# Writing the first stage and token block 0 out in ticks, in a one-core attention and two-MLP kernel on Trainium2

## The chip, the cores and the metric

The kernel runs on 1 core of one Trainium2 chip. The number that counts is the device time in microseconds (us) of one execution, as the median of several. The engines are TensorE (PE in the profile, with its weight loads as PEld), VectorE (DVE), ScalarE (ACT), GpSimd (POOL) and the queue engine SyncE (SP), which issues every DMA of this kernel in one row. Each engine works through its own list of instructions strictly in the order in which they stand there; engines wait for one another through semaphores.

## The reference

Three stages, one after the other, in float32 (inputs cut to what matters):

```python
# attention: q, k, v are (4 batches, 8 heads, 768 positions, 64)
k_sum = k.reshape(B, H, nb, 32, D).max(axis=3)      # 24 summary keys
v_sum = v.reshape(B, H, nb, 32, D).mean(axis=3)     # 24 summary values
scores_l = scale * q @ k^T, kept where |i - j| < 16, else -1e9
scores_s = scale * q @ k_sum^T + log(32)
a = softmax(concat[scores_l, scores_s]);  x = a @ concat[v, v_sum]
x = x.transpose(0, 2, 1, 3).reshape(3072, 512)
# first MLP: w1, w2, w3 are (512, 768), w_out is (768, 512)
x = max(max(x @ w1, x @ w2), x @ w3) @ w_out
# second MLP: w_in is (512, 2048), w_out2 is (2048, 512)
h = x @ w_in;  out = (h * tanh(softplus(h))) @ w_out2
```

The weights arrive as float64, and the kernel reads them as pairs of 32-bit words.

## The kernel before, in words

**Tokens.** The 3072 tokens are cut into 8 blocks of 384. A block is 3 attention units u (128 tokens each, two tiles of 64 queries), so block 0 is u = 0, 1, 2 and the kernel has 24 units, 6 to a batch. Block i's first MLP is 18 groups of 12 matmuls (`gemm1`: three products for each of 6 column slices f; the code calls their tiles hp, m, hh, hl) and then a part that multiplies by w_out (`gemm2`: tiles yp and y, stored to x2d).

**Precision.** Each float32 factor is split into a coarse and a fine part (xh and xl, hh and hl, two halves of each weight slot), and a product is three matmuls: coarse by coarse, coarse by fine, fine by coarse.

**Weight jobs.** The first MLP's weights are 24 pieces of 128x512 numbers. A job fetches a piece's words (`fetch`, a DMA of 512 KB into the tile words, 3 buffers), takes magnitudes on ACT (`size_of`, L177, tile wa), turns float64 words into a float32 and a rest on DVE (`narrow`, five instructions L185, L187, L190, L193, L195), rounds to the coarse part on ACT (L235), and forms the fine part. For the first 14 jobs (PEJOBS) PE adds the parts (L240 to L242, tile wp) and ACT copies the sum out (L243); for the last 10, DVE does it with two further instructions (L198 and L237). `run_job` moves the pipeline on by one: it finishes one job, fetches another, narrows a third and sizes a fourth. Jobs 1 to 18 are w1, w2, w3 by column slice; 19 to 24 are w_out.

**Attention.** A unit has five steps, made by `step(u)`: scores, row maximum and exponentials of u+1 (`s2`); a q transpose of u+2, with the preparation of keys of the next batch (`k_prep`, tiles tp, kst, ksum); first half of the transposes of u (`s3`, tiles ptp, pT) and normalisation of u+1 (`s2b`); preparation of the next batch's value means (`v_prep`, tiles vp, nat, stored to vsd) and the second half of s3; the output product of u (`s4`, tiles xp, xh, xl) and loads of keys for u+2. `KLOAD0` and `VLOAD0` say at which of batch 0's units the keys and values of batch 1 are loaded. Keys of later tiles come from a copy in DRAM, kTd, that `store_far` and `k_prep` write. The tile nat has 4 buffers, shared by q, k and v loads; y and m share one pair of buffers (tag my).

**Order.** The instructions are written in program order and a scheduler then places them on each engine by a simulated time, so two weight jobs may stand interleaved and later work may be pulled ahead. What steers it in the program is the order of the calls: the first stage runs 4 jobs among the first unit's work, and then one job after every second attention step:

```python
IB = ITEMS * BT // GT            # 15 attention steps to a block
while nstep < IB + 1:
    attend(nstep + 1)
    for _ in range(PER[nit % len(PER)]):     # PER = [1, 0]
        run_job()
    nit += 1
```

Each block's loop then takes its 22 groups one by one: in blocks 0 and 1 it calls `run_job` before each while there are jobs, then emits the group, then calls `attend(IB * (i + 1) + (IB * (n_ + 1)) // G + (AHEAD * min(n_ + 1, 8)) // 8)`, so that attention stands up to 19 steps beyond block i's own (AHEAD is 4) when the block ends.

Of the kernel before, what the change touches and what calls it, by code (L numbers as in the profile page):

```python
# [33 lines left out]
ITEMS = 5  # L34
PER = [1, 0]
AHEAD = 4
# [17 lines left out]
def tile_kernel(ctx, tc, q, k, v, w1, w2, w3, w_out, w_in2, w_out2, out):  # L54
# [88 lines left out]
    last = {"early": True}  # L143

# [53 lines left out]

    fetched, sized, narrowed = [], [], []

    def run_job(after=None):

        if narrowed:
            w, rest, done = narrowed.pop(0)
            done(w, rest)
        if jobs:
            src, done, parts = jobs.pop(0)
            fetched.append((fetch(src), done, parts))  # L210
        if sized:
            words, a, done, parts = sized.pop(0)
            narrowed.append((*narrow(words, a, parts), done))
        if fetched and (len(fetched) > 1 or not jobs):
            words, done, parts = fetched.pop(0)
            with tc.issue_after(after) if after else nullcontext():
                a = size_of(words)
            sized.append((words, a, done, parts))

    def busy():  # L220
        return bool(jobs or fetched or sized or narrowed)

# [5 lines left out]
    def into(tag, place, key):  # L228
        def done(w, rest):
            if tag not in slot_of:  # L230
                slot_of[tag] = wslot(tag)
            t = slot_of[tag]
            wa[key] = t, 2 * place
            h, l = t[:, 2 * place], t[:, 2 * place + 1]
            nc.scalar.copy(h, w)  # L235
            if rest is None:
                nc.vector.tensor_tensor(out=l, in0=w, in1=h.bitcast(F32), op=ALU.subtract)  # L237
                return
            sums = gps.tile([P, 512], F32, name="wp", tag="g")
            nc.tensor.matmul(sums, lhsT=ident, rhs=w, start=True, stop=False)  # L240
            nc.tensor.matmul(sums, lhsT=one_r, rhs=rest, start=False, stop=False)
            nc.tensor.matmul(sums, lhsT=neg_r, rhs=h, start=False, stop=True)  # L242
            nc.scalar.copy(l, sums)  # L243

        return done
# [13 lines left out]
    def keep(f, i):  # L259
        def done(w, _):  # L260
            h = stage.tile([P, 512], F32R, name="wr", tag="wr", bufs=AB)
            nc.scalar.copy(h, w)
            nc.vector.tensor_tensor(out=w, in0=w, in1=h.bitcast(F32), op=ALU.subtract)
            nc.sync.dma_start(out=w2d[f][:, 2 * i], in_=h.bitcast(F32))
            last["store"] = nc.sync.dma_start(out=w2d[f][:, 2 * i + 1], in_=w)

        return done
# [166 lines left out]

    def s2(u):

        t = u % NG
        kind = "first" if t == 0 else "last" if t == NG - 1 else "mid"
        mask = masks[kind]
        sc = [bank("sc") for r in range(2)]  # L440
# [8 lines left out]
        for p in range(NP):  # L449
            for e in reversed(range(GT)):  # L450
                for r in range(2):
                    d = slice(r * D, (r + 1) * D)
                    c = slice(e * QT, (e + 1) * QT)
                    nc.tensor.matmul(
                        sc[r][c, p, 0:KX], lhsT=qT[u % RQ][d, p, c], rhs=kT[(GT * u + e) % RK][d, p],
                        start=add, stop=add or p == NP - 1,
                    )
        s = ap2.tile([P, H, KX], F32, name="s", tag="s", bufs=SB)
        src = [x[:, :, 0:KX] for x in sc]
        if add:  # L460
# [10 lines left out]
        sm = ap2.tile([P, H], F32, name="esum", tag="esum")  # L471
        for h in range(H):
            r, p = divmod(h, NP)
            nc.scalar.activation(  # L474
                out=s[:, h], in_=src[r][:, p], func=AF.Exp, bias=nm[:, r, p : p + 1], accum_out=sm[:, h : h + 1]
            )
        rs = ap2.tile([P, H, 1], F32, name="rs", tag="rs")
        att_t[u] = (s, sm, rs)

# [44 lines left out]
    VLOAD = {0: [0], 1: [1], 2: [2], 3: [3, 4, 5], 4: [6, 7]}  # L524
    KLOAD0 = {1: [0, 1], 2: [2, 3], 3: [4, 5]}
    VLOAD0 = {1: [0], 2: [1], 3: [2], 4: [3, 4, 5]}

    def step(u):
# [5 lines left out]
        def first():  # L534
            if u == 1:
                store_far()
            for T in (GT * (u + 1), GT * (u + 1) + 1):
                if ok(u + 1):
                    load_v(T)
            if ok(u + 1):  # L540
                s2(u + 1)

        def second():
            if ok(u + 2):
                q_prep(*divmod(u + 2, NG))
            for g in more and kload.get(t - 1) or ():
                k_prep(b + 1, g)
            if ok(u + 3):
                load_nat("q", q, *divmod(u + 3, NG))
            for g in more and kload.get(t) or ():  # L550
                load_nat("k", k, b + 1, g)
# [7 lines left out]
        def fourth():  # L559
# [5 lines left out]
            for g in more and vload.get(t) or ():  # L565
                if b:
                    load_vsum(b + 1, *VP[g])
                else:
                    load_nat("v", v, 1, g)
            s3(u, 1)  # L570

        def fifth():
            s4(u)
            for T in (GT * (u + 2), GT * (u + 2) + 1):
                if ok(u + 2):
                    load_k(T)
# [47 lines left out]
    def gemm2(i, e):  # L624
# [14 lines left out]

        return [emit]  # L640


# [117 lines left out]
    vroom = [r[:, j].rearrange("p (h d) -> p h d", h=H) for r in vroom for j in range(4)]  # L760
    for g in range(NG):
        nat["k", 0, g] = t = room[g].rearrange("p (h d) -> p h d", h=H)
        nc.sync.dma_start(out=t, in_=k[0, :, g * P : (g + 1) * P, :].rearrange("h p d -> p h d"))
        if g == 2:
            load_nat("q", q, 0, 0)
    run_job()
    for g in range(NG):
        nc.sync.dma_start(out=vroom[g], in_=v[0, :, g * P : (g + 1) * P, :].rearrange("h p d -> p h d"))
        if g == 2:
            run_job()  # L770
    load_nat("q", q, 0, 1)
    for g in range(NG):
        k_prep(0, g, kst[g])
    for T in range(RK):
        load_k(T)
    q_prep(0, 0)
    run_job()
    s2(0)
    load_v(0)
    load_v(1)  # L780
    s2b(0)
    q_prep(0, 1)
    run_job()
    load_nat("q", q, 0, 2)
    vp = aps.tile([P, H, D], F32, name="vp", tag="a")
    for g in range(NG):
        mean_v(vp[0:NB].rearrange("p h d -> p (h d)"), vroom[g], g * NS, NB, g == 0, g == NG - 1)
    nc.scalar.copy(vr[0][0:NB], vp[0:NB])
    for t in vr[1:]:
        nc.gpsimd.tensor_copy(t[0:NB], vr[0][0:NB])  # L790

    steps = [it for u in range(NU) for it in step(u)]
    nstep = nit = 0

    def attend(upto):
        nonlocal nstep
        while nstep < min(upto, len(steps)):
            steps[nstep]()
            nstep += 1

    IB = ITEMS * BT // GT
    while nstep < IB + 1:
        attend(nstep + 1)
        for _ in range(PER[nit % len(PER)]):
            run_job()
        nit += 1

# [30 lines left out]
    early = 0  # L838
    for i in range(NBLK):
        groups = []  # L840
# [57 lines left out]
```

## Time and profile before

| what | value |
|---|---|
| median of 3 runs | 1119.14 us (1119.0 to 1120.24) |
| the profiled execution's own time | 1121.29 us |
| its span, first to last instruction | 1119.5 us |
| mean granted TensorE clock | 0.991 |
| PE busy | 1087.2 us, 97% of the span |
| DVE busy | 816.1 us, 73% |
| ACT busy | 548.6 us, 49% |
| DMA moved | 125.49 MB |

A timeline row reads: start in us, length in us, engine, line, operation, output<-inputs, shapes, count, and in brackets the idle time ahead of it with what ended it. A row of the table by stretches gives the busy time, with the number of instructions, of each engine. Matmul rows overlap, since matmuls are pipelined, so a matmul's price is the distance between starts. A PE that counts as busy isn't PE at its peak.

### The profile page before, as it was taken

The numbers are of one execution on the slowest core, as the hardware profiler recorded it, in microseconds if no ns is written. First come the engines' busy times: TensorE is split into PE (matmuls) and PEld (weight loads), VectorE is DVE, ScalarE is ACT, GpSimd is POOL, SyncE is SP. The second block draws the span as 40 slices with busy tenths as digits, with TensorE's granted clock in tenths as the row PEclk, the third lists the DMA queues.
The fourth block names the chain that finished last, engine by engine and source line by source line (L and its number), as shares of the span: only waits on it lengthen the run. The fifth ranks groups of instructions, "written<-read, shape, count | busy, mean of one in ns | idle before, by whom it ended". The sixth has DMA issues, their size and how long they took to land.

```text
span 1119.5 us, 18658 instructions
## 1 busy us (share of the span) xinstructions
PE 1087.2 (97%) x7004; PEld 986.9 (88%) x7004; DVE 816.1 (73%) x1623; ACT 548.6 (49%) x1336; POOL 77.4 (7%) x132
## 2 busy tenths in 40 slices
PE   6789989999999999999999999999999999999998
PEld 3468879999999899999999999989899998999987
DVE  5788953377887898942247887887878778787775
ACT  4676543345544555532135554545545454554543
POOL 3000021211114100100000000000000000000000
PEclk8989999999999999999999999999999999999999
DMA  9898772467888877412646010101001010000000
GB/s 239 199 248 230 170 193 63 136 155 197 247 224 253 200 228 190 152 37 71 233 178 248 20 37 1 57 1 29 29 1 58 1 44 14 15 29 1 29 1 29
DMA packets 179730, 125.49 MB, mean 112 GB/s; under 512 B 125048, under 2 KB 161400, under 8 KB 177592
## 3 DMA queue, kind: packets, MB, share of 16 engines
q1 hardware_dynamic: 179640, 124.30, 39.9%
q8 instruction: 55, 0.90, 0.3%
q14 instruction: 35, 0.29, 0.1%
HBM read 88.05 MB, written 35.05 MB: 110 GB/s over the span
## 4 chain that ended last, share of the span: by engine, by line
PE 75%; DVE 11%; ACT 6%; DMA 4%; issue 2%; SPq 1%; POOL 1%; ACTq 0%; POOLq 0%; DVEq 0%
PE up L692 8%; PE up L690 8%; PE acc L745 8%; PE up L691 8%; PE acc L746 8%; PE acc L747 8%; PE hp L599 5%; PE hp L600 5%; PE hp L601 5%; ACT s L474 3%; PE yp L633 2%; PE yp L634 2%; PE yp L635 2%; DMA kT<-kTd 1%; DVE words L190 1%
## 5 line engine op out<-in xcount | busy, mean ns | idle before, releaser
L708 ACT ACTIVATE r<-n,two 128x384 f32<-128x384 f32 x128 | 78.9, 616 | 155.3 <-DVE n L705 155.3
L599 PE MATMUL hp<-xh,a 128*128 128x384 f32 x384 | 133.6, 348 | 2.0 <-ACT y L637 2.0
L600 PE MATMUL hp<-xl,a 128*128 128x384 f32 x384 | 129.5, 337 | 0.0
L601 PE MATMUL hp<-xh,a 128*128 128x384 f32 x384 | 129.3, 337 | 0.0
L731 DVE TENSOR_TENSOR gl<-g,gh 128x384 fp32r<-128x384 f32 x128 | 71.4, 557 | 64.7 <-ACT gh L730 64.1
L701 ACT ACTIVATE e<-up 128x384 f32<-128x384 f32 x128 | 62.9, 492 | 97.3 <-PE up L692 96.6
L474 ACT ACTIVATE s<-s,nm 128x120 f32<-128x120 f32 x168 | 64.0, 383 | 45.1 <-DVE nm L467 45.1
L599 PEld LDWEIGHTS hp<-xh,a 128*128 128x128 f32 x384 | 72.7, 189 | 4.7 <-ACT y L637 2.4
L718 DVE TENSOR_TENSOR p<-up,r 128x384 f32<-128x384 f32 x128 | 70.5, 551 | 6.2 <-ACT r L709 6.2
L600 PEld LDWEIGHTS hp<-xl,a 128*128 128x128 f32 x384 | 72.7, 189 | 0.8 <-issue 0.5
L601 PEld LDWEIGHTS hp<-xh,a 128*128 128x128 f32 x384 | 72.7, 189 | 0.0
L723 DVE SCALAR_TENSOR_TENSOR g<-u,n 128x384 f32<-128x384 f32 x128 | 70.8, 553 | 0.9
L703 DVE TENSOR_SCALAR ep<-e 128x384 f32<-128x384 f32 x128 | 45.9, 358 | 34.8 <-ACT e L701 34.3
L721 DVE SCALAR_TENSOR_TENSOR u<-u,p 128x384 f32<-128x384 f32 x128 | 70.6, 552 | 0.4
L705 DVE SCALAR_TENSOR_TENSOR n<-e,ep 128x384 f32<-128x384 f32 x128 | 70.7, 552 | 0.3
L720 DVE SCALAR_TENSOR_TENSOR u<-n,r 128x384 f32<-128x384 f32 x128 | 70.2, 548 | 0.0
L730 ACT CAST gh<-g 128x384 fp32r<-128x384 f32 x128 | 64.2, 502 | 9.7 <-DVE g L723 9.7
L633 PE MATMUL yp<-hh,c 128*128 128x384 f32 x192 | 65.4, 346 | 3.5 <-ACT hh L618 1.9
L709 ACT ACTIVATE r<-r 128x384 f32<-128x384 f32 x128 | 67.1, 524 | 0.9
L599 PE MATMUL hp<-xh,b 128*128 128x384 f32 x192 | 67.4, 351 | 0.0
L611 DVE TENSOR_TENSOR m<-hp,m 128x384 f32<-128x384 f32 x48 | 26.5, 553 | 53.4 <-PE hp L601 48.7
L692 PE MATMUL up<-x2h,a 128*128 128x384 f32 x192 | 64.6, 337 | 0.0
(171 smaller groups left out, 2920.3 us busy)
## 6 DMA issues: line engine op xcount, KB each, us to landing
words<-in_moe_w_out SPq DMA_DIRECT2D x22, 512.0 KB, 4.5
words<-in_moe_w SPq DMA_DIRECT2D x18, 512.0 KB, 5.2
words<-in_moe_w_in SPq DMA_DIRECT2D x16, 512.0 KB
w2d<-wr SPq DMA_DIRECT2D x32, 256.0 KB, 2.7
w2d<-wa SPq DMA_DIRECT2D x32, 256.0 KB, 4.1
kT<-kTd SPq DMA_DIRECT2D x35, 192.0 KB, 5.1
vr<-in_v SPq DMA_DIRECT2D x35, 192.0 KB, 5.2
nat<-in_q SPq DMA_DIRECT2D x24, 256.0 KB, 4.5
```

The lines of the kernel that those rows point to most:

```text
L474: nc.scalar.activation(out=s[:, h], in_=src[r][:, p], func=AF.Exp, bias=nm[:, r, p : p + 1], accum_out=sm[:, h : h + 1])
L599: nc.tensor.matmul(pt[:, :n], lhsT=wh, rhs=xh[:, c, :n], start=(c == 0), stop=False)
L600: nc.tensor.matmul(pt[:, :n], lhsT=wh, rhs=xl[:, c, :n], start=False, stop=False)
L601: nc.tensor.matmul(pt[:, :n], lhsT=wl, rhs=xh[:, c, :n], start=False, stop=(c == KC - 1))
L633: nc.tensor.matmul(pt[:, :n], lhsT=wh, rhs=hh[:, :n], start=(f == 0), stop=False)
L690: nc.tensor.matmul(pt[:, :N2], lhsT=wh, rhs=xh[:, c], start=(c == 0), stop=False)
L691: nc.tensor.matmul(pt[:, :N2], lhsT=wh, rhs=xl[:, c], start=False, stop=False)
L692: nc.tensor.matmul(pt[:, :N2], lhsT=wl, rhs=xh[:, c], start=False, stop=(c == KC - 1))
L708: nc.scalar.activation(out=r, in_=d["n"], func=AF.Ln, bias=two[:, 0:1])
L745: nc.tensor.matmul(o, lhsT=gh[:, c], rhs=w[:, 2], start=(f == 0), stop=False)
L746: nc.tensor.matmul(o, lhsT=gh[:, c], rhs=w[:, 3], start=False, stop=False)
L747: nc.tensor.matmul(o, lhsT=gl[:, c], rhs=w[:, 2], start=False, stop=(f == NF2 - 1))
```

## The change

The first stage and block 0 are written out by hand. A new context, `in_order`, links every instruction on an engine to the one traced before it on that engine, so inside it the scheduler may not reorder; it holds from the first load up to the end of block 0 (SP's DMAs included). A weight job is split into five calls: `fetch_next`, `size_next`, `narrow_next`, `round_next` (coarse part, and PE's sum where there is one) and `close_next` (fine part), and `s2` into `scores`, `largest` and `exps`. In the first stage these stand between single attention steps: 5 jobs are narrowed before the tick loop, in which block 0's remaining 21 pieces of work (three groups of gemm1 stand ahead of the loop) are taken one to a tick, with one `run_job` and some attention steps before each. Block 0's second product is cut by f, not by output slice (`gemm2_slices`), so that each slice needs one w_out job. `attend` ends block 0 at step 30. Loads of batch 1's keys and values start one unit later, and `in_order` ends before block 1, whose loop is as it was.

```diff
+    @contextmanager
+    def in_order():
+        traced = nc.cur_bb.bb.instructions
+        n = len(traced)
+        yield
+        latest = {}
+        for i in traced[n:]:
+            if i.engine in latest:
+                tc.add_manual_dep(
+                    i, latest[i.engine].name,
+                    mybir.DependencyInfo(mybir.DependencyClass.NoSync, mybir.DependencyReason.DATA),
+                    reason="in_order",
+                )
+            latest[i.engine] = i
...
     def run_job(after=None):
+        old = bool(narrowed)
+        if old:
+            round_next()
+        fresh = bool(fetched)
+        fetch_next()
         if sized:
+            narrow_next()
+        late = old and rounded[0][1]
+        if old and not late:
+            close_next()
+        if fresh:
             with tc.issue_after(after) if after else nullcontext():
+                size_next()
+        if late:
+            close_next()
...
-    VLOAD0 = {1: [0], 2: [1], 3: [2], 4: [3, 4, 5]}
+    KLOAD0 = {2: [0, 1], 3: [2, 3], 4: [4, 5]}
+    VLOAD0 = {2: [0], 3: [1], 4: [2], 5: [3, 4, 5]}
...
                     load_nat("v", v, 1, g)
+            if u == NG - 1:
+                for g in VLOAD0[t]:
+                    v_prep(1, g)
             s3(u, 1)
...
+    def gemm2_slices(i):
+        def part(f):
+            if f == 0:
+                pts.extend(gps.tile([P, 512], F32, name="yp", tag="g") for e in range(KC))
+            w, at = wa[4, f]
+            hh, hl = hhl[i, f]
+            for e, pt in enumerate(pts):
+                wh, wl = w[:, at, e * P : (e + 1) * P], w[:, at + 1, e * P : (e + 1) * P]
+                nc.tensor.matmul(pt[:, :n], lhsT=wh, rhs=hh[:, :n], start=(f == 0), stop=False)
+                nc.tensor.matmul(pt[:, :n], lhsT=wh, rhs=hl[:, :n], start=False, stop=False)
+                nc.tensor.matmul(pt[:, :n], lhsT=wl, rhs=hh[:, :n], start=False, stop=(f == NF1 - 1))
+                if f == NF1 - 1:
+                    y = g2.tile([P, MAXT * QT], F32, name="y", tag="my", bufs=2)
+                    nc.scalar.copy(y[:, :n], pt[:, :n])
+                    nc.sync.dma_start(out=x2d[i][:, e, :], in_=y[:, :n])
...
+    with in_order():
...
+        round_next()
+        s4(2)
+        scores(3)
+        first_groups = [g for f in range(NF1) for g in gemm1(0, f)] + gemm2_slices(0)
+        first_groups.pop(0)()
+        narrow_next()
+        largest(3)
+        close_next()
+        exps(3, 0)
+        exps(3, 1)
+        first_groups.pop(0)()
...
+        s2b(3)
+        first_groups.pop(0)()
+        nstep = IB
+        tick = 0
+        while first_groups:
+            if busy():
+                run_job()
+            attend(IB + (tick * IB) // 22)
+            first_groups.pop(0)()
+            tick += 1
+        attend(2 * IB)
...
-    for i in range(NBLK):
+    for i in range(1, NBLK):
```

Three places show how instructions moved. The first is DVE in the middle of block 0, in the weight jobs (wa, words and wr are a job's tiles, m and hl the MLP's). Before:

```order
L185 TENSOR_SCALAR wa<-wa 128x512
L187 TENSOR_SCALAR wa<-wa 128x512
L611 TENSOR_TENSOR m<-hp,m 128x384
L366 TENSOR_REDUCE ksum<-tp 128x4x4
L190 SCALAR_TENSOR_TENSOR words<-words,wa 128x512
L185 TENSOR_SCALAR wa<-wa 128x512
L193 TENSOR_SCALAR wa<-words 128x512
L187 TENSOR_SCALAR wa<-wa 128x512
L195 SCALAR_TENSOR_TENSOR wa<-words,wa 128x512
```

and in the change, from the loop's first ticks:

```order
L674 TENSOR_TENSOR m<-hp,m 128x384
L678 TENSOR_TENSOR hl_746<-m,hh_745 128x384
L200 TENSOR_SCALAR wa<-wa 128x512
L202 TENSOR_SCALAR wa<-wa 128x512
L205 SCALAR_TENSOR_TENSOR words<-words,wa 128x512
L208 TENSOR_SCALAR wa<-words 128x512
L210 SCALAR_TENSOR_TENSOR wr<-words,wa 128x512
L200 TENSOR_SCALAR wa<-wa 128x512
```

The five instructions of one job, which had another job's or other work between them, now stand in a row, and hl stands right behind the m that it is made from. The second place is the DMA queue. Before, in the middle of block 0, the last loads of batch 1's values stood among the weight fetches:

```order
L303 DMA nat<-in_v 128x8x64
L368 DMA kTd_175<-kst 512x1x128
L303 DMA nat<-in_v 128x8x64
L167 DMA words<-in_moe_w_out 128x1024
L318 DMA vsd_179<-nat 4x8x64
L368 DMA kTd_175<-kst 512x1x128
L303 DMA nat<-in_v 128x8x64
```

and in the change, at the end of block 0 (x2d takes block 0's result y):

```order
L182 DMA words<-in_moe_w_out 128x1024
L182 DMA words<-in_moe_w_in 128x4x256
L719 DMA x2d_182<-y 128x384 x4
L358 DMA vsd_179<-nat 4x8x64
L343 DMA nat<-in_v 128x8x64 x3
L358 DMA vsd_179<-nat 4x8x64
```

The three loads moved behind block 0's four stores. The third place is ACT where block 0 ends and block 1 begins. Before:

```order
L474 ACTIVATE s,esum<-s,nm 128x120 x8
L637 COPY y<-yp 128x384 x2
L496 COPY pT<-ptp 120x512 x2
L363 COPY kst<-tp 128x512
L637 COPY y<-yp 128x384 x2
L607 COPY m<-hp 128x384
```

and in the change:

```order
L272 CAST c_1558<-wa 128x512
L549 COPY pT<-ptp 120x512
L718 COPY y<-yp 128x384 x4
L357 COPY nat<-vp 4x512 x4
L549 COPY pT<-ptp 120x512
L570 CAST xh<-xp 128x4x128
L666 COPY m<-hp 128x384
```

Between y and the first m of block 1 there now stand four value means, a transpose copy and the last xh of block 1's input. PE has the same row there: the last slice's yp matmuls, then vp x4, ptp, xp, and then hp, block 1's first product.

More of the change, by code (lines that the diff above doesn't have):

```diff
@@ L2 @@
 import struct
[L3 removed]
+from contextlib import ExitStack, contextmanager, nullcontext
 import concourse.bass as bass
@@ L199, in narrow, with fetch_next @@
         return a, None
[L201 to L207, printed above, removed]
+    fetched, sized, narrowed, rounded = [], [], [], []
+    def fetch_next():
         if jobs:
@@ L210, in run_job, with size_next, narrow_next, round_next @@
             fetched.append((fetch(src), done, parts))
-        if sized:
[L212 to L215, printed above, removed]
+    def size_next():
+        words, done, parts = fetched.pop(0)
+        sized.append((words, size_of(words), done, parts))
+    def narrow_next():
+        words, a, done, parts = sized.pop(0)
+        narrowed.append((*narrow(words, a, parts), done))
+    def round_next():
+        w, rest, done = narrowed.pop(0)
+        rounded.append((done(w, rest), rest is not None))
+    def close_next():
+        rounded.pop(0)[0]()
+    def run_job(after=None):
+        old = bool(narrowed)
[3 more added lines that the diff above has]
+        fetch_next()
+        if sized:
+            narrow_next()
[3 more added lines that the diff above has]
+        if fresh:
             with tc.issue_after(after) if after else nullcontext():
-                a = size_of(words)
-            sized.append((words, a, done, parts))
+                size_next()
+        if late:
+            close_next()
     def busy():
-        return bool(jobs or fetched or sized or narrowed)
+        return bool(jobs or fetched or sized or narrowed or rounded)
     jobs = []
@@ L242, in done @@
             nc.tensor.matmul(sums, lhsT=neg_r, rhs=h, start=False, stop=True)
-            nc.scalar.copy(l, sums)
+            return lambda: nc.scalar.copy(l, sums)
         return done
@@ L545, in second @@
                 q_prep(*divmod(u + 2, NG))
-            for g in more and kload.get(t - 1) or ():
+            for g in more and not (b == 0 and t == NG - 1) and kload.get(t - 1) or ():
                 k_prep(b + 1, g)
@@ L573, in fifth @@
             s4(u)
+            if b == 0 and t == NG - 2:
+                for g in KLOAD0[t]:
+                    k_prep(1, g)
             for T in (GT * (u + 2), GT * (u + 2) + 1):
@@ L640, in gemm2 @@
         return [emit]
+    def gemm2_slices(i):
+        n = sizes[i] * QT
+        pts = []
+        def part(f):
[12 more added lines that the diff above has]
+                    nc.sync.dma_start(out=x2d[i][:, e, :], in_=y[:, :n])
+        return [lambda f=f: part(f) for f in range(NF1)]
     N2 = 384
@@ L760, in tile_kernel @@
     vroom = [r[:, j].rearrange("p (h d) -> p h d", h=H) for r in vroom for j in range(4)]
[L761 to L790, printed above, removed]
     steps = [it for u in range(NU) for it in step(u)]
-    nstep = nit = 0
+    nstep = 0
     def attend(upto):
```

145 lines of the change are left out of this document (123 added, 22 removed).

## The prediction

> **What bounds the kernel now.** I read the slices of the span first: they show where PE isn't full.
>
> ```profile
> PE   6789989999999999999999999999999999999998
> ```
>
> A slice is 28 us, so the time that a new order can win back lies in the first six slices; after them PE is busy and sets the pace. Next, three PE rows: block 0's first product, the last matmuls of its second product, and block 1's first product.
>
> ```profile
> 71.74 0.34 PE L599 MATMUL hp<-xh,a 128*128 128x384 f32 x1
> ...
> 154.27 0.96 PE L635 MATMUL yp<-hh,c 128*128 128x384 f32 x4
> 157.25 0.44 PE L599 MATMUL hp<-xh,a 128*128 128x384 f32 x1 [2.02 <-ACT y L637]
> ```
>
> Block 0 ends on PE at 155.2 and block 1 starts 2.0 later, at 157.25. From there on everything is PE's work, so the change is worth what it does to two numbers: when block 1 starts, and how much PE work is done by then. What holds block 0 back is DVE, which the stretches from 0 to 58 and from 58 to 152.6 show, first DVE alone, then the L190 step, of which each weight job has one:
>
> ```profile
> 58.00:152.60 94.60, 85.19 (x158) 0.96 0.90 209
> ...
> 0.00:58.00 58.00, 5.53 (x8) 0.94 0.89 221
> 58.00:152.60 94.60, 11.00 (x16) 0.96 0.90 209
> ```
>
> By 58 us 8 jobs are narrowed; the other 16 keep DVE at 85.2 of 94.6 us.
>
> **Part 1: when the tick loop starts.** The change has 5 jobs narrowed before its loop, and attention goes first. But PE's order has the scores of unit 3 ahead of block 0's first product, and these need keys that go out to DRAM and back. Before:
>
> ```profile
> 38.52 3.71 SPq L376 DMA_DIRECT2D kTd<-room  x4
> ...
> 54.68 1.05 PE L454 MATMUL sc<-kT,qT 64*64 64x120 f32 x32 [0.19 <-DMA kT<-kTd]
> ```
>
> The way from the first store to the scores took 16.2 us. In the change the stores stand behind the sixth fetch, which waits for job 3 to be rounded; I put them at 38 again, and the way at 12.5: between stores and key loads SP has one q load now, where two k loads and a weight fetch stood as well, some 4 us of issuing in all. Scores of unit 3: 50.5. From there one chain: the matmuls 1.05, the row maximum on DVE, eight exponentials on ACT, the normalisation, and f = 0's m and hl, with these prices:
>
> ```profile
> L467 DVE TENSOR_REDUCE nm<-s 128x8 f32<-128x960 f32 x6 | 6.9, 1144 | 0.0
> L366 DVE TENSOR_REDUCE ksum<-tp 128x16 f32<-128x512 f32 x7 | 4.8, 682 | 0.1
> L463 DVE TENSOR_TENSOR s<-sc,mask_mid 128x480 f32<-128x480 f32 x6 | 3.7, 648 | 0.0
> L485 DVE TENSOR_TENSOR s<-s,rs 128x960 f32<-128x960 f32 x3 | 3.5, 1157 | 0.1
> L518 DVE TENSOR_TENSOR xl<-xp,xh 128x512 fp32r<-128x512 f32 x5 | 3.4, 685 | 0.5 <-ACT xh L517 0.5
> ...
> L474 ACT ACTIVATE s<-s,nm 128x120 f32<-128x120 f32 x168 | 64.0, 383 | 45.1 <-DVE nm L467 45.1
> ```
>
> A score unit on DVE is 2 x 0.65 + 1.14 = 2.4, eight exponentials 3.1, the normalisation 1.5 with its two small helpers, m and hl 1.6: the loop's first job starts on DVE at 50.5 + 1.05 + 2.4 + 3.1 + 1.5 + 1.6 = 60. The ends I keep: 52 (stores at 34, landings quick) and 66 (the old 16.2, and PE at a lower clock).
>
> **Part 2: DVE in the loop.** 19 jobs are left, 9 whose parts PE adds (five DVE steps) and 10 that DVE finishes (seven). In the new order a job's steps follow one another and each needs the one before it. The trace has both kinds:
>
> ```profile
> 53.28 0.42 DVE L185 TENSOR_SCALAR wa<-wa 128x512 f32<-128x512 f32 x1
> 53.74 0.43 DVE L187 TENSOR_SCALAR wa<-wa 128x512 uint32<-128x512 uint32 x1
> 54.20 0.69 DVE L190 SCALAR_TENSOR_TENSOR words<-words,wa 128x512 uint32<-128x512 uint32 x1
> 54.92 0.43 DVE L193 TENSOR_SCALAR wa<-words 128x512 uint32<-128x512 uint32 x1
> ...
> 125.76 0.42 DVE L185 TENSOR_SCALAR wa<-wa 128x512 f32<-128x512 f32 x1
> 126.10 0.42 DVE L193 TENSOR_SCALAR wa<-words 128x512 uint32<-128x512 uint32 x1
> 126.43 0.42 DVE L187 TENSOR_SCALAR wa<-wa 128x512 uint32<-128x512 uint32 x1
> 126.77 0.68 DVE L195 SCALAR_TENSOR_TENSOR wa<-words,wa 128x512 f32<-128x512 uint32 x1
> 127.37 0.68 DVE L190 SCALAR_TENSOR_TENSOR words<-words,wa 128x512 uint32<-128x512 uint32 x1
> ```
>
> Start to start, a step that feeds the next takes 0.46 (53.28 to 53.74) or 0.72 (54.20 to 54.92); one that stands ahead of another job's step takes 0.34 (125.76 to 126.10) or 0.60 (126.77 to 127.37). So a five-step job is 0.46 + 0.46 + 0.72 + 0.46 + 0.60 = 2.7, a seven-step one 3 x 0.46 + 2 x 0.72 + 2 x 0.60 = 4.0, and the 19 are 9 x 2.7 + 10 x 4.0 = 64. Beside them stand 3 score units (7.3), 2 normalisations (3), 6 ksum (4.1), 2 xl (1.4) and the m, m, hl of 5 slices (15 x 0.55 = 8.3): 24, less a tenth for starts that overlap, 22. Together 86.
>
> The Trainium skill, in VectorE: DVE Perf Modes, "The DRAIN you can't avoid", says that a chain with a semaphore after each step takes exactly as long as one without. By that rule the new row of steps costs nothing; the rows above disagree by 0.12 a step, and the measurement decides. With the rule the sum would be 10 us lower (9 x 4 + 10 x 5 = 86 links).
>
> Three stalls come on top. The rows are a wait of hl for ACT's hh, where hl stands right behind m as it now always does, and on PE two sums of a job and two steps of a product:
>
> ```profile
> 167.44 0.56 DVE L619 TENSOR_TENSOR hl<-m,hh 128x384 fp32r<-128x384 f32 x1 [0.58 <-ACT hh L618]
> ...
> 35.62 1.07 PE L240 MATMUL wp<-words,ident 128*128 128x512 f32 x2
> ...
> 36.98 1.06 PE L240 MATMUL wp<-words,ident 128*128 128x512 f32 x2
> ...
> 98.50 0.33 PE L601 MATMUL hp<-xh,a 128*128 128x384 f32 x1
> 98.67 0.33 PE L599 MATMUL hp<-xh,a 128*128 128x384 f32 x1
> ```
>
> Five times 0.58 is 2.9. Once hh stands on ACT behind unit 4's eight exponentials, which take 3.1 and start as m does: 2.9 more. And in the first nine ticks PE is the longer one: 12 matmuls at 0.17 make 2.1, a job's sum takes 1.4 (35.62 to 36.98), and attention in those ticks, by the prices of Part 4, is near 0.8 a tick: 4.3, against 2.7 + 0.55 + 0.75 = 4.0 on DVE: 9 x 0.3 = 2.7. I take 8.5 for the three (ends 0 and 14). The last fine part waits for its rounding (0.7), and the last slice is 12 matmuls (2.1). End of block 0 on PE: 60 + 86 + 8.5 + 0.7 + 2.1 = 157.3, against 155.2: **+2.1**. The early start buys nothing because DVE has three more jobs ahead of it and dearer ones.
>
> **Part 3: from block 0's end to block 1's start.** Now block 1's first product needs the last xh, and that stands behind a queue of waits: four y copies, where the third needs the first one's store landed (one pair of buffers); SP holds batch 1's last three value loads behind the y stores, and the third of these needs a nat buffer that is free only when unit 5's first mean has been stored; PE has four means ahead of the last transposes. Rows:
>
> ```profile
> 156.74 0.83 ACT L637 COPY y<-yp 128x384 f32<-128x384 f32 x2
> ...
> 160.23 0.93 ACT L637 COPY y<-yp 128x384 f32<-128x384 f32 x2 [0.39 <-DMA x2d<-y]
> ...
> 105.43 0.28 SPq L318 DMA_DIRECT2D vsd<-nat  x1
> ...
> 107.75 0.39 SPq L303 DMA_DIRECT2D nat<-in_v  x1
> ...
> nat<-in_q SPq DMA_DIRECT2D x24, 256.0 KB, 4.5
> ...
> L306 PE MATMUL vp<-nat,mean x10: 592/592/593, 86.3 to 123.3; 128*4 128x512 f32 x10
> ...
> L317 ACT COPY nat<-vp x6: 558/571/575, 65.8 to 125.1; 4x512 f32<-4x512 f32 x6
> ```
>
> With T as the last slice's end: the first y ends at T - 1.0, the third starts 3.0 later (157.2 to 160.23), T + 2.0, and the fourth ends at T + 3.0; the mean's copy T + 3.5; its store lands 2.3 later (105.43 to 107.75), T + 5.8; the load lands after 3.5 (ends: 2.3, as the small store, and 4.5), T + 9.3; the mean 1.0, its copy and pT 0.57 each, the output product 1.15, xh 0.57: T + 13.2, and 0.2 until xl is there too (the first four matmuls need only xh). So 13.4 where it was 2.0: **+11.4**. Nothing hides it: PE's row has no other work there.
>
> PE's clock falls in such a gap, as early in the run, where PE waits (busy 2.29 of 5 us):
>
> ```profile
> 20.00:25.00 5.00, 2.29 (x4) 1.14 (x5) 3.71 (x6) 1.19 (x3) 0.00 (x0) 0.65 0.99 263
> ```
>
> At 0.65 for the first 3 us I take **+1.0** (ends 0 and 3). The Trainium skill, TensorE: Matmul & The Clock Gate, "Part 1: The HAM clock gate", has half rate after an idle window of 3.4 us until one is busy: by it the term would be 1.7.
>
> **Part 4: work that is done later.** Before, 34 attention steps were called by the end of block 0, now 30. By the built order, PE has done 9 scores, 7 output products, 24 transposes of loads and 16 of probabilities (in fours) when block 1 starts; now 7, 6, 20 and 12. Their prices:
>
> ```profile
> 143.85 1.15 PE L508 MATMUL xp<-pT,vr 120*64 120x64 f32 x30
> ...
> 153.04 0.60 PE L352 MATMUL tp<-ident,nat 128*128 128x128 f32 x4
> 153.47 1.04 PE L494 MATMUL ptp<-ident,s 128*120 128x128 f32 x8
> ```
>
> 2 x 1.05 + 1.1 + 4 x 0.5 + 4 x 0.45 = 7.0, which block 1, full on PE, now has to take: **+7.0**. The end of block 1 has the same number of steps in both, so nothing comes back.
>
> **Sum.** +2.1 + 11.4 + 1.0 + 7.0 = +21.5 on the profiled execution's own 1121.3, 1.9%. The median of the runs is 1119.1; with the same step it becomes 1140.6. I say **1140**.
>
> **The rivals.** *Dependent steps cost no more than free ones* (the drain rule above). DVE's rows in the crowded part speak against it, since the gap of 0.12 is in each pair. It gives 21.5 - 10 = +11: 1130. Chance 0.13.
>
> *Weights come late.* In the loop a fetch may go out only when the job three before it is rounded, and stands on SP among loads that wait for PE. Two ticks are 9 us, the way is about 1 us of issue, a landing of 4.5 or somewhat more (the 256 KB load of Part 3; a fetch has twice that) and 0.7 of sizing: there is cover, but DMA is already at 0.9 of its share (windows above). If landings grow by 2 us, some ten ticks wait 1 us each: +31, 1150. Chance 0.12.
>
> *DVE starts early and never waits.* If unit 3's keys came so early that the loop started on DVE by 45, and no stall of Part 2 came up, block 0 would end at 45 + 86 + 2.8 = 134, 2.8 being the last two terms of Part 2: 134 - 155.2 + 11.4 + 1.0 + 7.0 = -2, 1117. It decides from a start at 47 downwards. For it speaks that only 5 jobs stand among the work of units 0 to 3, where 8 were done by 58 us; against it that the chain behind unit 3's scores alone is 9.6 us long and its keys would have to be there at 35, before the stores of Part 1 have even left. Chance 0.08.
>
> **How the numbers follow.** Forecast 0.67, with its own range 1130 to 1151 (start of the loop 52 to 66, tail 12 to 15). The whole range, 1125 to 1154, takes in the first two rivals. A measurement here can tell 0.2%, 2.2 us. Faster 0.07, same 0.05, slower 0.88: the first two are the third rival and half as much again for what I haven't seen.
>
> **What would show it.** On PE: block 0's first product near 52 (was 71.7), the last slice ending at 150 to 163, then four vp matmuls and about 13 us before block 1's hp, with a granted clock near 0.65 behind it. On DVE: L200 to L210 0.46 and 0.72 apart. On SP: three nat<-in_v behind four x2d. Wrong would be: a gap under 6 us, or block 0 ending before 140.

## The result, and the profile after

The changed kernel takes 1172.4 us (median of 4 runs, 1170.76 to 1177.35), the kernel before 1119.69 beside it: a ratio of 1.0474 with a 95% interval of 1.0438 to 1.051, 53 us slower. Direction and order of events were as forecast, the size was not: +21 was forecast, outside whose range (1125 to 1154) this lies. The profiled execution of the changed kernel was the longest of the four (1177.35 us, span 1175.6), so differences read from its trace add up to 56 and not to 53.

First the page of the changed kernel, its PE row and that of the granted clock in 40 slices (29 us each):

```profile
PE   7788557999999989999999999999999999999998
PEclk9989777999999989999999999999999999999999
```

Slices 5 to 7 (118 to 206 us), the second half of block 0's loop and its end, are now at 5 to 7 tenths, and the clock falls there to 0.7. Then PE's rows of the timeline at the same three places as before: block 0's first product, the last matmul of its last slice, block 1's first product.

```profile
52.93 0.45 PE L658 MATMUL hp<-xh,a 128*128 128x384 f32 x1
...
184.73 0.34 PE L715 MATMUL yp<-hh,c 128*128 128x384 f32 x1
199.97 0.62 PE L658 MATMUL hp<-xh,a 128*128 128x384 f32 x2 [0.69 <-ACT xh L570]
```

Block 0's first product comes 19 us earlier (52.93 for 71.74), yet its end comes 30 us later and block 1 starts at 199.97 for 157.25, 42.7 later. DVE's loop, from its first narrowing to its last fine part, in the table by stretches (PE, PEld, DVE, ACT, POOL; then clock, DMA share, GB/s), and the first and last row of it:

```profile
62.47:178.95 116.48, 81.98 (x486) 66.90 (x487) 85.44 (x155) 50.08 (x123) 0.86 (x2) 0.83 0.54 141
...
62.47 0.42 DVE L200 TENSOR_SCALAR wa<-wa 128x512 f32<-128x512 f32 x1
...
178.26 0.69 DVE L274 TENSOR_TENSOR c<-wa,c 128x512 fp32r<-128x512 f32 x1 [0.30 <-ACT c L272]
```

DVE is busy 85.4 of 116.5 us: it has the work that I counted, and stands idle for 31 us beside it. What it waited for there, from the list of waits (us in total, times, longest), and below the waits of ACT for the one key tile and for the weight words in the same loop:

```profile
DVE ksum L406 <- ACT kst L403: 10.0, 5, 2.8
DVE hl L678 <- ACT hh L677: 8.4, 6, 3.2
DVE m L670 <- PE hp L660: 5.4, 3, 4.0
...
ACT wa L192 <- DMA words<-in_moe_w: 9.7, 3, 5.9
ACT kst L403 <- DMA kTd<-kst: 8.3, 3, 2.9
```

The first line was in no term of mine. k_prep has one tile kst; two groups of keys are prepared one behind the other, so the second copy on ACT waits until the first one's store to DRAM has landed, ksum on DVE waits for that copy, and all weight jobs stand behind ksum.

The rest of the difference lies behind block 1's start. A block's end is taken as the start of its last y copy on ACT. Here are those of blocks 1, 2, 4 and 7, before and after:

```profile
218.46 0.48 ACT L637 COPY y<-yp 128x384 f32<-128x384 f32 x1 [0.72 <-PE yp L635]
281.06 0.49 ACT L637 COPY y<-yp 128x384 f32<-128x384 f32 x1
410.01 0.48 ACT L637 COPY y<-yp 128x384 f32<-128x384 f32 x1 [0.55 <-PE yp L635]
584.81 0.48 ACT L637 COPY y<-yp 128x384 f32<-128x384 f32 x1 [0.46 <-PE yp L635]
```

```profile
266.19 0.48 ACT L696 COPY y<-yp 128x384 f32<-128x384 f32 x1 [0.36 <-PE yp L694]
331.31 0.50 ACT L696 COPY y<-yp 128x384 f32<-128x384 f32 x1
466.42 0.49 ACT L696 COPY y<-yp 128x384 f32<-128x384 f32 x1
640.83 0.48 ACT L696 COPY y<-yp 128x384 f32<-128x384 f32 x1 [0.46 <-PE yp L694]
```

| stretch | before | after | difference |
|---|---|---|---|
| start to block 1's first product | 157.25 | 199.97 | +42.7 |
| block 1 | 61.2 | 66.2 | +5.0 |
| blocks 2 to 4 | 191.6 | 200.2 | +8.7 |
| blocks 5 to 7 | 174.8 | 174.4 | -0.4 |

The +8.7 in blocks 2 to 4 is a loss at a place where I had looked for nothing. Part of it belongs to this one execution: in the thirteen other traces below whose blocks 2 to 4 have the changed text, they take 197.1 to 199.1 us.

### The profile page after: what moved, and what is told of

Same layout as the page of the kernel before. It is cut to its first block, busy times and chain, and to the rows that moved or that the text cites. A ratio compares the mean times of both kernels' runs of the same rounds, so it can differ in the third digit from the quotient of the medians.

```text
span 1175.6 us, 18669 instructions
## 1 busy us (share of the span) xinstructions
PE 1105.0 (94%) x7004; PEld 998.8 (85%) x7004; DVE 820.4 (70%) x1623; ACT 548.1 (47%) x1336; POOL 78.2 (7%) x132
## 4 chain that ended last, share of the span: by engine, by line
PE 69%; DVE 6%; DMA 4%; ACT 3%; issue 2%; POOL 0%; SPq 0%; ACTq 0%; DVEq 0%; POOLq 0%
PE up L773 8%; PE up L771 8%; PE acc L826 8%; PE up L772 8%; PE acc L827 8%; PE acc L828 8%; PE hp L658 5%; PE hp L659 5%; PE hp L660 5%; PE yp L692 2%; PE yp L693 2%; PE yp L694 2%; ACT s L521 1%; PE xp L561 1%; DVE wa L301 1%
## 5 line engine op out<-in xcount | busy, mean ns | idle before, releaser
L658 PE MATMUL hp<-xh,b 128*128 128x384 f32 x192 | 68.3, 356 | 2.1 <-ACT b L272 2.1
L660 PE MATMUL hp<-xh,b 128*128 128x384 f32 x192 | 65.4, 341 | 0.5 <-DVE b L274 0.4
L659 PE MATMUL hp<-xl,b 128*128 128x384 f32 x192 | 65.1, 339 | 0.0
```

What stands on the lines that cost most here:

```text
L658: nc.tensor.matmul(pt[:, :n], lhsT=wh, rhs=xh[:, c, :n], start=(c == 0), stop=False)
L659: nc.tensor.matmul(pt[:, :n], lhsT=wh, rhs=xl[:, c, :n], start=False, stop=False)
L660: nc.tensor.matmul(pt[:, :n], lhsT=wl, rhs=xh[:, c, :n], start=False, stop=(c == KC - 1))
```

## The experiments

Three theories came first for the loop. Late words: SP, in one fixed row, stands at a wait, and weight words behind it come late (a rival of the prediction). One key buffer: the kst wait just shown. Fixed compute order: an engine whose row is fixed waits where the scheduler would have put other work.

**No fixed order at all** (e1_free).

```diff
-        for i in traced[n:]:
+        for i in ():
```

> The changed program's text, word for word, with in_order linking nothing, so that the scheduler places every instruction again. Three theories for the 25 us by which the tick loop came out longer than I forecast (62.5 to 184.9 us on PE). Late words: SP, in one fixed row, stands at a wait and the weight words behind it come late. One key buffer: two k_prep in a row share one kst, so that the second's copy waits for the first's store. Fixed compute order: an engine in a fixed order waits where another piece of work was ready. Here all three waits can be stepped around, so each of them gives block 1's first product near 175 instead of 200 and some 1147 us. If instead the rewritten text itself is the price (five jobs narrowed early, loads one unit later, 30 attention steps, slices by f, the last value means in front of unit 5's output), block 1's first product stays at 190 or later and the time at 1162 or more.

1126.8 us, ratio 1.0072 (1.0045 to 1.0099): 45.6 us of the 53 are the fixed order's. On PE, block 0's last slice and block 1's first product:

```profile
150.75 0.86 PE L715 MATMUL yp<-hh,c 128*128 128x384 f32 x4
...
154.02 0.59 PE L658 MATMUL hp<-xh,a 128*128 128x384 f32 x2
```

This is 20 us better than I expected of it, and block 1 even starts 3 us earlier than in the kernel before. The rewritten text costs some 8 us all the same, and not in block 0: blocks 2 to 4 take 198.9 us here (218.82 to 417.70, the starts of the last y copies), for 191.6.

**SP's row free; the key tiles; more word buffers** (e2_spfree, e3_kst, e4_words), each alone in the changed kernel. `kst` is the list of batch 0's six key tiles, `spare` two pieces of the weight slot c0, which no job writes before the 19th.

```diff
-            if i.engine in latest:
+            if i.engine in latest and i.engine != nc.sync.engine:
```

> in_order for PE, DVE, ACT and POOL as in the change, SP's row of transfers left to the scheduler. Late words: ACT's 9.7 us of waits for words in the loop and the waits of DVE for PE's products behind them go; block 1's first product near 188 instead of 200, time 1160. One key buffer: the 8.3 us in which kst waits for its store stay, so at most 3 us are won: 1169 to 1172. Fixed compute order: nothing, 1172.

```diff
+        if b == 1:
+            st = kst[g]
-        if st is None:
+        elif st is None:
             st = ap1.tile([P, NP, P], F32, name="kst", tag="kst")
```

> The changed kernel, in which batch 1's key preparation writes into batch 0's six key tiles (free by then) and not into the one buffer kst. One key buffer: kst no longer waits for kTd stores (8.3 us in 3 waits) nor ksum on DVE for kst (10.0 us in 5); block 1's first product near 190, time 1162. Late words: the stores also leave SP earlier, 3 us at most: 1169. Fixed compute order: another wait takes its place, 1172.

```diff
-        words = stage.tile([P, 1024], U32, name="words", tag="words")
+        j = len(taken)
+        taken.append(j)
+        if j < 18 and j % 5 >= 3:
+            words = spare[j % 5 - 3]
+        else:
+            words = stage.tile([P, 1024], U32, name="words", tag="words")
```

> The changed kernel with two more buffers for the weight words in the loop's first 13 jobs (in a weight slot that is not yet in use), so that a fetch needs the job five before it and not the one three before. SP's 52 us of waiting at fetches for ACT, PE and DVE go for the greater part. Late words: ACT's 9.7 us of waits for words go, block 1's first product near 190, time 1162. One key buffer: no gain, 1172. Fixed compute order: no gain, 1172.

1173.7 us (1.0491, 1.0456 to 1.0525), 1163.2 (1.0398, 1.0374 to 1.0422) and 1174.2 (1.0495, 1.0469 to 1.0521). Only the key tiles win, 9.2 us, as that theory said. DVE's waits with them:

```profile
DVE hl L680 <- ACT hh L679: 7.1, 6, 3.2
DVE m L672 <- PE hp L662: 5.4, 3, 2.5
DVE ksum L408 <- ACT room L405: 2.2, 2, 1.7
```

ksum's wait falls from 10.0 to 2.2, and block 0's last product comes 11.9 us earlier in the trace (172.88 for 184.73). With SP's row free ksum's wait rises instead, to 14.9 in the same list. With more word buffers the waits of ACT for words shrink from 9.7 us to 6.5, and SP's waits move from the fetches to the next thing in its row (its wait for kst at the kTd stores, 17.1 us in 4 of the loop, becomes 30.0 in 4):

```profile
DVE ksum L406 <- ACT kst L403: 14.9, 5, 5.1
```

```profile
ACT wa L197 <- DMA words<-in_moe_w: 6.5, 1, 6.5
...
SPq L413 <- ACT kst L408: 30.0, 4, 15.2
```

Neither run takes the longest single wait for words away (5.9 us in the changed kernel, 2.9 with SP's row free, 6.5 with more buffers), so they show only that shortening these waits by some 3 us brings nothing. The free order settles the rest: there ACT waits 7.8 us in 6 for words (60 to 155 us), nearly as long as the 9.7 here, and block 0 still ends over 30 us earlier. Late words fall as the cause of the long loop.

**The tail** (e5_tail): the last three value means behind unit 5's output.

```diff
-            if u == NG - 1:
-                for g in VLOAD0[t]:
-                    v_prep(1, g)
             s3(u, 1)
...
             s4(u)
+            if u == NG - 1:
+                for g in VLOAD0[t]:
+                    v_prep(1, g)
...
-        attend(2 * IB)
+        attend(2 * IB - 1)
+    attend(2 * IB)
```

> The changed kernel, with the last three value means of batch 1 made behind unit 5's output and not ahead of its last transposes, and that last attention step outside the fixed order. If the gap between block 0's last product and block 1's first (184.9 to 199.97 us on PE, 15 us) is the chain of Part 3 (y copies, loads behind them, a store, a load, a mean), it shrinks to the y copies, pT, the output product and xh, about 6 us: 9 us won, 1163. If the y copies and the last normalisation alone hold unit 5's output, the gap stays above 12 and the time above 1169.

1167.5 us (1.0427, 1.0408 to 1.0446), 4.9 won. The gap:

```profile
182.17 0.34 PE L715 MATMUL yp<-hh,c 128*128 128x384 f32 x1
...
187.27 0.62 PE L658 MATMUL hp<-xh,a 128*128 128x384 f32 x2 [0.68 <-ACT xh L570]
```

From 15.2 us, start to start, to 5.1: the chain of Part 3 was the gap. Only half of it reached the medians. The three means stand on PE in block 1 now, 0.95 each, 2.9 together, which I forgot in the expectation, and block 1 is 3.5 longer in this trace than in the changed kernel's (69.8 for 66.2); the rest, some 2 us, is within the two intervals, which just touch.

**One compute engine free at a time** (e6_dvefree, e7_actfree, e8_pefree), each by the edit of e2_spfree with another engine's name.

> in_order for every engine but DVE, whose row the scheduler places. DVE's idle time in the loop is 31 us (62.5 to 179.0, busy 85.4). If DVE's own fixed row is what loses it (an instruction that waits for ACT or PE stands ahead of a ready one), some 15 us come back: block 1's first product near 185, 1157. If the stalls are handed round between the engines, each in its own fixed row, freeing one engine brings 5 us at most: 1167 or more.

> in_order for every engine but ACT. If ACT's row is the cause (hh behind eight exponentials, the sizing that waits for a close, kst behind its store, all of them ahead of ready copies), DVE's waits for hh (8.4 us) and for kst (10.0) shrink by half or more: some 12 us, 1160. If the stalls are handed round between the rows, 5 us at most: 1167 or more.

> in_order for every engine but PE. PE stands idle in the loop as well (busy 82 of 116.5 us), behind roundings (9.1 and 4.2 us), keys (7.1) and fine parts (5.2). If PE's row is the cause, DVE's waits for PE's products (7.0 us) go, and with them most of those that follow: 10 us, 1162. If the stalls are handed round between the rows, 5 us at most: 1167 or more.

1164.1 us (1.0399, 1.0363 to 1.0434), 1167.4 (1.0425, 1.0403 to 1.0447) and 1174.7 (1.0489, 1.0469 to 1.0509): 8.3, 5.0 and nothing won, together far from 45.6 (the interval behind the 5.0 just touches the changed kernel's). With DVE free, its wait for ksum shrinks to 3.2 us, and another grows that was 1.3 in the changed kernel:

```profile
DVE wa L200 <- ACT wa L192: 12.6, 10, 4.8
```

DVE now has nothing to narrow, since ACT, in its fixed row, has not sized the next job. The waits are handed round between the rows.

**Only SP fixed** (e17_only_sp).

```diff
-            if i.engine in latest:
+            if i.engine in latest and i.engine == nc.sync.engine:
```

> in_order for SP alone, the compute engines' rows left to the scheduler. If the rows of PE, DVE and ACT together are what costs 46 us (freeing one at a time gave 8, 5 and nothing), the time is that with no fixed order, 1126 to 1130. If SP's fixed row costs by itself once the others are free to use what arrives, 1135 or more.

1146.4 us (1.0224, 1.0202 to 1.0245), 19.6 above the free order and 26.0 below the changed kernel: the second case, SP's fixed row costs by itself.

```profile
154.85 0.96 PE L715 MATMUL yp<-hh,c 128*128 128x384 f32 x4 [0.28 <-DVE c L274]
...
171.19 0.62 PE L658 MATMUL hp<-xh,a 128*128 128x384 f32 x2 [0.69 <-ACT xh L570]
```

This parts the cost in two. The loop ends 4.1 us later than in the free order (154.85 for 150.75), so the 30 us that it lost in the changed kernel (184.73) are the compute engines' rows. But the gap is 16.3 from the start of that row, where the free order has 3.3: the value loads behind the y stores on SP are enough to make the tail. PE has the last means ahead of the last transposes in the free order too, but the last value load leaves SP at 141.64 there, ten us ahead of the y stores (from 151.63). With only SP's row free (e2_spfree) the gap is 13.3:

```profile
186.92 2.74 PE L346 MATMUL vp<-nat,mean 128*4 128x512 f32 x6
194.28 1.86 PE L346 MATMUL vp<-nat,mean 128*4 128x512 f32 x2 [4.62 <-DMA nat<-in_v]
```

Two of the three loads are early there. But the fixed compute rows keep the first means behind the last product on PE (186.92) and their copies behind the y copies on ACT (188.81), so the last load leaves only at 191.02, after their stores, and PE waits 4.62 us for it. SP's row alone makes most of the tail, and so do the compute engines' rows alone, which is why freeing SP's wins nothing.

**34 attention steps in the free order** (e9_free_more), and with the key tiles (e10_free_more_kst).

```diff
-        attend(2 * IB)
+        attend(2 * IB + 4)
```

> The changed text with in_order linking nothing (1126.8 us, 7.6 over the kernel before, with block 1's first product 3 us earlier than there) and 34 attention steps called by the end of block 0, as before the change, instead of 30. If the rest of the loss is the work that is done later (Part 4, +7.0), the time comes to 1119 to 1121. If that work costs nothing, or if the four steps only push block 1's start back by what they save, it stays at 1125 to 1128.

> The same, with batch 1's key preparation in batch 0's six key tiles. If the one key buffer costs also where the order is free (kst waits 7.0 us for stores there, DVE 3.0 for kst), 2 to 3 us less than the run with 34 steps: 1117. If a free order fills such waits with other work, the same as that run, 1120.

1126.4 us (1.0057, 1.0041 to 1.0074) and 1123.8 (1.0041, 1.0029 to 1.0054). The four steps win nothing that can be told, and the key tiles' 2.6 us lie within the two intervals. The four calls moved no work either: PE has 549 matmuls in block 1 in both traces, with the 30 steps of e1_free and with the 34. So this run does not say what the moved work costs, only that the number of calls is not what the 8 us of the rewritten text hang on.

**The group ahead of attention in a tick** (e12_swap), and this with the key tiles and the tail (e13_kst_tail_swap).

```diff
-            attend(IB + (tick * IB) // 22)
             first_groups.pop(0)()
+            attend(IB + (tick * IB) // 22)
```

> The changed kernel, all rows fixed, in which a tick has its matmul group ahead of its attention steps and not behind them. So hh no longer stands on ACT behind the eight exponentials of its tick. If hl's wait for hh (8.4 us in 6) is a cost of its own, 3 to 5 us are won: 1168. If waits are handed round between fixed rows, another takes its place: 1171 to 1174.

> The changed kernel, all rows fixed in block 0, with batch 0's key tiles for batch 1's keys (9.2 us won alone), the last value means behind unit 5's output (4.9 won alone) and the group ahead of attention in a tick. If the shares add up: 1158, less what the third one brings. If the waits are handed round, so that a share won in one place is lost in another: 1163 or more. In neither case is the fixed order as quick as the free one (1126.8).

1172.2 us (1.0479, 1.0458 to 1.05) and 1161.4 (1.0376, 1.0357 to 1.0395). The swap alone shows the handing round at its plainest:

```profile
DVE ksum L406 <- ACT kst L403: 15.6, 5, 7.4
DVE m L670 <- PE hp L660: 4.8, 3, 2.4
DVE hl L678 <- ACT hh L677: 3.5, 5, 1.0
```

hl's wait falls from 8.4 to 3.5, as meant, and ksum's rises from 10.0 to 15.6. The three edits together win 11.0, where the shares (9.2, 4.9 and, for the swap, nothing) add up to 14.1.

**The order inside run_job from block 2 on** (e14_free_old, e15_fixed_old, e16_before_new). The change also turned run_job's own order round, for all jobs: before, a job was rounded and closed (fine part, two stores) ahead of the next fetch and the next narrowing; after, it is closed behind the narrowing. In the two kernels of the changed text the old order is put back for the later jobs; in the kernel before, the new one is put in.

```diff
     def run_job(after=None):
+        if after:
+            if narrowed:
+                round_next()
+                close_next()
+            fetch_next()
+            if sized:
+                narrow_next()
+            if fetched and (len(fetched) > 1 or not jobs):
+                with tc.issue_after(after):
+                    size_next()
+            return
```

> The changed text with no fixed order, 34 attention steps and batch 0's key tiles (1123.8 us), and from block 2 on run_job in its old order: a job is rounded and closed with its stores ahead of the fetch and of the next narrowing. If that order is what blocks 2 to 4 lose (block 2's start to block 4's end took 198 us there and 191.6 in the kernel before), some 5 us come back: 1119 or less. If something else loses them, 1123 to 1125.

> The run with the fixed order, batch 0's key tiles, the means behind unit 5's output and the group first (1161.4), with the old order of run_job from block 2 on. If that order is the loss in the later blocks, 1156; if not, 1160 to 1163.

> The kernel before with one edit: from block 2 on run_job in the change's order (round, fetch, narrow, close with the stores, size). Up to there every engine's row is as in the kernel before. If this order is the later loss, 1123 to 1125; if not, 1118 to 1120.

e14_free_old 1117.2 us (0.9979, 0.9968 to 0.999), 6.6 less than e10_free_more_kst; e15_fixed_old 1154.7 (1.0304, 1.0288 to 1.0319), 6.7 less than e13_kst_tail_swap; e16_before_new 1127.9 (1.0071, 1.0055 to 1.0087), 7.8 more than the kernel before. One edit, three times the same size, and it shows where it should: blocks 2 to 4 take 191.1 to 191.8 us in the three traces with the old order (before, e14_free_old, e15_fixed_old), 198.3 in e16_before_new and 197.1 to 200.2 in the others. Its way is in the waits of blocks 2 to 4 (219 to 411 before, 219 to 419 in e16_before_new), before:

```profile
PE ptp L494 <- DVE s L463: 1.5, 1, 1.5
...
DVE wa L185 <- ACT wa L177: 3.1, 5, 1.4
```

and with the new order:

```profile
PE ptp L518 <- DVE s L487: 2.3, 1, 2.3
PE ptp L518 <- DVE xl L542: 0.6, 1, 0.6
...
DVE wa L185 <- ACT wa L177: 10.4, 9, 2.9
...
ACT wa L177 <- DMA w2d<-wa: 5.8, 6, 1.9
```

A tile wa is closed later, so its store leaves later; the next sizing on ACT waits for that store (two buffers), DVE waits 10.4 us for sizings where it waited 3.1, and at 370 us it is late with a unit's scores for PE. This order of waits is read off one trace and not shown by an edit of its own. On PE the 6.7 us by which blocks 2 to 7 are longer in that trace are 2.8 of idle time and 3.9 in which nearly the same number of matmuls (2855 for 2856) takes longer; 2.7 of these lie in the stretch of the last section, where the clock is halved. e14_free_old is quicker than both kernels: the changed text, with the fixed order, the later run_job order and the one key tile taken out and the four steps put back. Its lead of 0.2% is about what can be told at all.

## Why the prediction was right or wrong

Own terms against the trace, on the profiled execution:

| term | forecast | measured | from |
|---|---|---|---|
| loop's start on DVE | 60 | 62.5 | first narrowing of the loop |
| DVE's work in it | 86 | 85.4 | busy time |
| stalls, with the last fine part | 9.2 | 31.0 | 116.48 less 85.44 |
| last fine part to block 0's end | 2.1 | 6.1 | 178.95 to 184.73 + 0.34 |
| gap to block 1 | 13.4 | 14.9 | 185.07 to 199.97 |
| moved work and clock | 8.0 | 5.0 | block 1 |
| blocks 2 to 7 | 0 | 8.3 | last y copies |

The differences, 2.5 + 21.3 + 4.0 + 1.5 - 3.0 + 8.3 with 21.3 for the loop's length (116.5 for 95.2), make 34.6; with the forecast's 21.5 this is the 56 of the spans.

**Part 1 held**: 52.93 for "near 52", and a loop that starts 2.5 late.

**Part 2 failed at one step**, "I take 8.5 for the three (ends 0 and 14)": with the last fine part's 0.7 that is 9.2, and 31.0 were measured. The DVE work was right, and the price of a step that feeds the next was in every job:

```profile
106.88 0.42 DVE L200 TENSOR_SCALAR wa<-wa 128x512 f32<-128x512 f32 x1
107.33 0.43 DVE L202 TENSOR_SCALAR wa<-wa 128x512 uint32<-128x512 uint32 x1
107.79 0.69 DVE L205 SCALAR_TENSOR_TENSOR words<-words,wa 128x512 uint32<-128x512 uint32 x1
108.52 0.43 DVE L208 TENSOR_SCALAR wa<-words 128x512 uint32<-128x512 uint32 x1
```

0.46 and 0.73 start to start, so the first rival (the rule in the Trainium skill, VectorE: DVE Perf Modes, "The DRAIN you can't avoid") falls here as it did in the trace of before.

The stalls were mis-sized for two reasons. I listed those that I could see a row for, and missed that one key tile, harmless while other work could step past it, becomes a stall in a fixed row: ksum's 10.0 us, 9.2 us of time by e3_kst. The two that I did list came out longer as well: hl's wait for hh 8.4 for 5.8, DVE's wait for PE's products 6.2 (5.4 and 0.8) for 2.7. With 3.7 in smaller waits the list of DVE's waits comes to 28.3 of the 31.0. And with every row fixed a delay is handed on. Taking one wait or one row out (e2, e4, e7, e8, e12) gave back from nothing to 5 us, DVE's row alone 8.3, the compute engines' rows together 26.0. Which wait starts the chain stays open. ACT's longest waits in the loop are sizings that wait for an earlier job's fine part (15.8, 7.8 and 4.3 us in 8; the tile wa has two buffers), and no run took these out.

The way from the last fine part to block 0's end was 4.0 longer than forecast: PE had waited 3.3 us for a coarse part (to 177.28), two slices of 12 matmuls were left and not one, and the granted clock was 0.58 and 0.57 in the two stretches from 176 to 184.

**Part 3 held** as a mechanism, as e5_tail shows, and nearly in size: 14.9 for 13.4. That the size came so near is in part luck. PE did not wait for the third load: it waited for the first (5.32 us, to 191.35) and then ran the three means without a pause, some 1.7 us each at a granted clock of 0.50 (191.3 to 197), where I had one mean of 1.0 at the end. And I did not see that SP's row and the compute rows make the tail each alone.

**Part 4 held, and the clock term had the wrong sign.** Together they came to 5.0 in block 1, where 8.0 was forecast. PE's matmuls in block 1, before and after, are 64 and 128 for scores, 64 and 96 for output products, 24 and 40 for transposes of loads, 14 and 30 for those of probabilities: the 2 scores, 1 product and 4 groups of each kind that I had counted at 7.0. What I had not read is that the kernel before already lost clock behind its own gap of 2.02 us (granted clock in the last column but two; it is 0.89 from 161 to 163 and then 1.00), and that the changed kernel starts block 1 at full clock:

```profile
157.25:159.00 1.75, 1.75 (x7) 1.75 (x8) 0.03 (x1) 1.28 (x3) 1.55 (x1) 0.72 1.17 332
159.00:161.00 2.00, 2.00 (x8) 2.00 (x8) 0.69 (x1) 1.36 (x3) 1.36 (x3) 0.50 0.43 158
```

```profile
199.97:205.00 5.03, 5.03 (x36) 4.70 (x40) 0.77 (x2) 0.48 (x1) 0.00 (x0) 1.00 1.06 191
```

Before, 1.75 x 0.28 + 2 x 0.50 + 2 x 0.11 = 1.7 us were lost there. So the term is not +1.0 but -1.7, and 7.0 - 1.7 = 5.3 is near the 5.0.

**Left out altogether** was the order inside run_job in the blocks behind block 0. The diff shows it, and I read it as part of the tick loop; the loop from block 1 on is as it was only in its own text, since the `run_job` that it calls is not. It costs 6.6 to 7.8 us, in three pairs of runs. "From there on everything is PE's work" was true of the kernel before, and I took it for the changed one without looking at who feeds PE there.

**The rivals.** Weights come late would have given 1150 by a wait for words; such waits came to 9.7 us, but in the free order they come to 7.8 us with a loop 30 us shorter, and shortening them (e2_spfree, e4_words) won nothing. The early start came only to 62.5, well behind the 47 from which it would have decided.

The changed kernel's loss of 53 us is then, by differences of runs that are good to some 3 us: 45.6 the fixed order, and 7.1 the text, about the price of run_job's order alone. Of the 45.6, freeing the compute engines' rows first gives 26.0, and SP's row after them 19.6, most of it the tail. The key tile's 9.2 seem to belong to the 26.0: with only SP's row fixed DVE waits 0.3 us for it (60 to 155 us). The shares depend on which row is freed first: SP's, freed first, gives nothing.

## What to carry to other kernels

A hand-written order on every engine can turn a wait of one into idle time of all, and this one did: before fixing it, list every tile with a single buffer and every store in the rows, since a wait that other work steps past in the old trace costs nothing there. Free the rows one by one and all together: where one alone gives little and all together much, the delay is handed round, and pricing one wait says little about what removing it wins. Before adding a loss of clock for a gap, look whether the old kernel pays one at the same place. And an edit of a helper changes every place that calls it: look at each caller's stage in the profile, those that look settled included.

## What was not expected of the hardware

A short wait on PE can cost twice. In e16_before_new PE waits 0.59 and 2.28 us within 4 us, and then the granted clock (last column but two) is halved for about 5 us though PE has work:

```profile
367.75 0.62 PE L518 MATMUL ptp<-ident,s 128*120 128x128 f32 x4 [0.59 <-DVE xl L542]
370.64 1.11 PE L518 MATMUL ptp<-ident,s 128*120 128x128 f32 x4 [2.28 <-DVE s L487]
...
371.00:374.00 3.00, 3.00 (x12) 3.00 (x11) 2.93 (x6) 1.02 (x5) 0.00 (x0) 0.50 1.08 318
374.00:377.00 3.00, 3.00 (x12) 3.00 (x12) 2.54 (x6) 3.00 (x15) 0.29 (x1) 0.60 0.25 58
377.00:380.00 3.00, 3.00 (x43) 2.75 (x43) 2.34 (x4) 1.94 (x5) 1.50 (x1) 1.00 0.76 264
```

That is 3 x 0.50 + 3 x 0.40 = 2.7 us on top of the 2.9 waited. The 1.7 us lost behind the gap of 2.02 us at block 1's start in the kernel before are of the same kind. The kernel before waits 1.47 us for the scores here, and that left the clock at 1.00 in the 10 us behind it:

```profile
366.67 0.66 PE L494 MATMUL ptp<-ident,s 128*120 128x128 f32 x4 [1.47 <-DVE s L463]
...
370.00:380.00 10.00, 9.74 (x108) 8.90 (x107) 8.74 (x17) 5.74 (x18) 1.79 (x1) 1.00 0.81 209
```

The Trainium skill, TensorE: Matmul & The Clock Gate, "Part 1: The HAM clock gate", speaks of half the rate after an idle window of about 3.4 us; here two waits of 2.9 us together, with four small matmuls between them, were enough, and so was the one of 2.02 us.
